# Linear attention and two expert layers on one core: zero products ahead of the first pair, its k in two transfers, and the negative sign first

## The chip, the cores and the metric

One core of one Trainium2 chip runs the whole program. The metric is device time in microseconds (us) of one execution. The engines are TensorE (PE, with PEld its weight loads), VectorE (DVE), ScalarE (ACT), GpSimd (POOL) and SyncE (SP), whose queue issues nearly all transfers.

## The reference

q, k and v have 4 batches of 8 heads, 576 tokens and 64 columns; w_phi has 64 rows and 128 columns.

```python
def phi(x):
    proj = np.einsum('bhsd,df->bhsf', x, w_phi)
    proj = proj - np.max(np.abs(proj), axis=-1, keepdims=True)
    return np.concatenate([np.exp(proj), np.exp(-proj)], axis=-1)
q_p, k_p = (phi(q), phi(k))
kv = np.einsum('bhsf,bhsd->bhfd', k_p, v)
z = np.sum(k_p, axis=2)
num = np.einsum('bhsf,bhfd->bhsd', q_p, kv)
den = np.einsum('bhsf,bhf->bhs', q_p, z)[..., None] + 1e-06
attn = num / den
...
h = x @ w_in                       # first layer, 2304 x 512 by 512 x 2048
x = np.maximum(0.01 * h, h) @ w_out
h = x @ w_in                       # second layer
out = (h * (1.0 / (1.0 + np.exp(-h)))) @ w_out
```

## The kernel before

The 32 heads are worked as 16 pairs, two heads beside each other on the 128 partitions. The first 8 pairs are "full": their products are in full float32. The later 8 are split into a high and a low part and made beside the first layer. The first layer goes over five tiles of 460 or 462 tokens (t) and over 16 blocks of hidden columns (c); each h is made of high and low parts by three products (emit_h, line 533) and goes into four output banks (emit_y, line 553). The second layer is made of seven products for each two-by-two block (lines 613 and 689).

A full pair goes through these steps. load_qk (line 110) and load_v issue on SP the transfers of kr (512 tokens of k), kt (its last 64 tokens), qr (q) and va (v). s_pk makes k's features with w_phi, two banks of two products each (line 180), and s_pkt those of the tail (line 195); each product leaves two records in the trace. k_features takes the largest absolute value (DVE, line 156) and subtracts it (line 157); then ACT makes exp(-x) into sign slot 1 (line 166) and exp(x) in place into sign slot 0 (line 167), for four token groups at once and, with the tail, for five. s_pq makes q's features (line 217), copies them to p (ACT, lines 223 and 225) and lets POOL find the largest value m over the partitions (line 227); s_eq subtracts it (DVE, line 239) and makes both exponentials of q (ACT, lines 243 and 244). These come in two parts of the tokens, 0 and 1. s_kv makes the key-value products of both signs, one of line 262 and eight of line 268 for each, and ACT copies the bank to KV (line 273). num_full makes the numerators and the denominator (line 302, in part 1 also line 305); DVE adds 1e-6 (line 311), takes the reciprocal (312) and makes x (313); PE transposes x (lines 316 and 320), and ACT and DVE split it into the first layer's high and low input (lines 287 and 126).

In between, the weights of the first layer are prepared: raw is a block of w_in or w_out as 64-bit words (line 411), narrowed by ACT (lines 420 and 421) and DVE (lines 422 to 425) and split into wih and wil, or wo (lines 429 and 126). Three buffers hold raw; two hold kr, three kt, qr and va. Four PSUM banks are called ps_a and four ps_y.

What sets the order: the program calls the steps by a table of due times, OFF0 for the full pairs, five units a pair, with prep_wi put in at four places (PRE). The framework that records the kernel then schedules all instructions and gives each engine a fixed order of its own. So a few instructions more can give every engine another order. A transfer has one of eight semaphores, DMAHW0 to DMAHW7, in turn; the one that takes a semaphore again waits until the transfer that had it has landed.

Of the kernel before, what the change touches and what calls it, by code (L numbers as in the profile page):

```python
# [8 lines left out]
F32 = mybir.dt.float32  # L9
# [10 lines left out]
def tile_linear_attention_ffn_ffn(ctx: ExitStack, tc: tile.TileContext, q, k, v, w_phi, w_in1, w_out1, w_in2, w_out2, out):  # L20


    nc = tc.nc
# [7 lines left out]
    S0 = 512  # L31
# [12 lines left out]
    gp = ctx.enter_context(tc.tile_pool(name="gp", bufs=2))  # L44
# [7 lines left out]
    def at(shape, dt, tag):  # L52
        return att_pool[0].tile(shape, dt, tag=tag, bufs=AB[0].get(tag, 1), name=tag)

    def ps(tag):

        return psp.tile([128, 512], F32, tag=tag, name=f"ps_{tag}")
# [3 lines left out]
    def aps(step):  # L61

        return ps("y" if PRO[0] and step in ("pq", "kv", "nt") else "a")
# [9 lines left out]
    def make_consts():  # L73
        for c in (slice(0, 2 * F), slice(2 * F, 3 * F + 128)):
            nc.scalar.dma_start(wc[:, c], w_phi[:, c])
        first = [const.tile([128, 2], F32, name=f"first{i}") for i in range(2)]
        nc.gpsimd.memset(first[0], 0.0)
        nc.gpsimd.partition_all_reduce(first[1], first[0], 128, bass_isa.ReduceOp.absmax)
# [30 lines left out]
    def load_qk(i):  # L109

        st = P[i]
        st["kr"] = at([128, S0], F32, "kr")
        st["kt"] = at([128, 128], F32, "kt")
        st["qr"] = at([128, S], F32, "qr")
        nc.sync.dma_start(st["kr"], k[i, :, 0:S0])
        nc.sync.dma_start(st["kt"], k[i, :, S0:])
        nc.sync.dma_start(st["qr"], q[i])

# [6 lines left out]
    def sub(out_, x, h):  # L125
        nc.vector.tensor_tensor(out_, x, h.bitcast(F32), op=ALU.subtract)  # L126

    def full(i):
        return i < NFULL
# [126 lines left out]
    def s_kv(i):  # L256
        st = P[i]
        ke, va = st["ke"], st["va"]
        pv = aps("kv")[:, 0 : 4 * NKV].rearrange("p (s j d) -> p s j d", s=2, j=2)
        vf = va.rearrange("p c d -> p (c d)")  # L260
        for s in range(2):
            nc.tensor.matmul(
                pv[:, s, :, 0 : D + 1], ke[:, 8, s, :], va[:, 8:10], start=True, stop=False, skip_group_check=True
            )
            for j in range(2):
                for c in range(4):
                    w = (4 * j + c) * (D + 1)
                    nc.tensor.matmul(  # L268
                        pv[:, s, j], ke[:, 2 * c + j, s, :], vf[:, w : w + NKV], start=False, stop=(j == 1 and c == 3), skip_group_check=True
                    )  # L270
        if full(i):
            st["KV"] = at([128, 2, 2, NNUM], F32, "KV")
            nc.scalar.activation(st["KV"], pv[:, :, :, 0 : NNUM], AF.Copy)
            return
        h, l = st["KVH"], st["KVL"] = at([128, 2, 2, 2, D], F32R, "KVH"), at([128, 2, 2, 2, D], F32R, "KVL")
        for j in range(2):
            kv_, z_ = pv[:, :, j, 0:D], pv[:, :, j, D : D + 1].to_broadcast([128, 2, D])
            for slot, sr in ((j, kv_), (1 - j, z_)):
                nc.scalar.activation(h[:, j, :, slot, :], sr, AF.Copy)
                sub(l[:, j, :, slot, :], sr, h[:, j, :, slot, :])  # L280
# [80 lines left out]
    def s_num(a):  # L361
        return lambda i: (num_full if full(i) else num_split)(i, a)

    W, WP = 8.0, 5.0
    fns = dict(
        lq=load_qk, lv=load_v, sp=s_split, pq0=s_pq(0), pq1=s_pq(1),
        pk0=s_pk(0), pk1=s_pk(1), pkt=s_pkt, eq0=s_eq(0), eq1=s_eq(1), kv=s_kv, num0=s_num(0), num1=s_num(1), fin0=s_fin(0), fin1=s_fin(1),
    )
    FIN = 16
# [19 lines left out]
    def run_att(until, tile_=None):  # L389
        while seq and (seq[-1][0] < until or (tile_ is not None and missing(tile_))):  # L390
            if seq[-1][1] == NFULL and AB[0] is ABUFS0:
                att0_ctx.close()
                att_pool[0] = att_ctx.enter_context(tc.tile_pool(name="att1", bufs=1))
                AB[0] = ABUFS1
            _, i, n_ = seq.pop()
            f = fns[n_]
            f(i)
# [76 lines left out]
    def prep_wi(layer, c):  # L474
        raw = load_wi(layer, c)
        h = wp.tile([128, KD, 128], F32R, tag="wih", bufs=NC, name="wih")
        l = wp.tile([128, KD, 128], F32R, tag="wil", bufs=NC, name="wil")
        split64(raw, h.rearrange("p k f -> p (k f)"), l.rearrange("p k f -> p (k f)"))
        wi[layer, c] = (h, l)
# [235 lines left out]
    def pace(s):  # L715

        return SLOW * min(s, NC) + FAST * max(0, s - NC)

    make_consts()
    for c in range(PRE):  # L720
        run_att(13.52 + 11.07 * c)
        prep_wi(0, c)
# [52 lines left out]
    for u, gs in GROUPS.items():  # L775
        for i, ps_ in enumerate(gs):
# [7 lines left out]
            if last:  # L784
                y = y3_ops(u, list(ps_))
# [87 lines left out]
```

## Time and profile before

| | us |
|---|---|
| median of 3 runs | 964.19 |
| lowest, highest | 962.32, 964.91 |
| the profiled execution | 963.19 |
| its span, first to last instruction | 961.4 |

The profile is of one execution. A row of the timeline gives start and length in us, the engine, the line, the tiles written and read, the number of merged records and, in brackets, how long the engine had stood idle and what ended that. The windows give, for a stretch, its length and the busy time of each engine with the number of instructions, then the clock that TensorE was granted (1.00 is 2.4 GHz), the mean busy share of the sixteen DMA engines and what they moved.

### The profile page before, as it was taken

The page shows a single profiled execution, that of the slowest core. Times are in us where ns is not written, and L with a number is a line of the kernel's source. Part 1 is how long each engine was busy: PE and PEld are TensorE (multiplying, and loading weights), DVE is VectorE, ACT ScalarE, POOL GpSimd, SP SyncE. Part 2 cuts the span into 40 slices and gives each one's busy share as a digit, 9 for nine tenths or more (in the row PEclk, how much of TensorE's full clock was granted, in tenths as well). Part 3 has the DMA queues.
Part 4 walks back from the last instruction along what each step waited for, and adds up shares of the span by engine and source line. Part 5 has one row for each costly group of instructions (what it writes and reads, how often), then busy time and mean ns, then how long its engine had stood idle before and what let it go on. Part 6 is the DMA issues. An engine that isn't in the chain of part 4 may idle for free.

```text
span 961.4 us, 15778 instructions
## 1 busy us (share of the span) xinstructions
PE 943.6 (98%) x5376; PEld 883.6 (92%) x5376; DVE 649.1 (68%) x1279; ACT 597.2 (62%) x1224; POOL 78.4 (8%) x56
## 2 busy tenths in 40 slices
PE   7999999999999999999999999999999999999998
PEld 6878888889999998888888999999999999999998
DVE  6677799986666655278777767778762595624853
ACT  6568687877777776466655556566554565544553
POOL 3434200201111111000000000000000000000000
PEclk9999999999999999999999999999999999999999
DMA  6333477874334232299999999896988778987784
GB/s 223 99 105 102 154 243 256 284 267 129 116 112 116 78 128 79 86 355 384 356 337 334 368 356 346 299 349 239 319 287 294 243 234 264 300 281 222 251 278 138
DMA packets 102384, 226.13 MB, mean 235 GB/s; under 512 B 15008, under 2 KB 24992, under 8 KB 102304
## 3 DMA queue, kind: packets, MB, share of 16 engines
q1 hardware_dynamic: 102016, 224.86, 69.9%
q8 instruction: 43, 0.70, 0.3%
q14 instruction: 37, 0.30, 0.1%
q10 hardware_dynamic: 288, 0.26, 0.1%
HBM read 177.82 MB, written 47.22 MB: 234 GB/s over the span
## 4 chain that ended last, share of the span: by engine, by line
PE 79%; DMA 8%; DVE 6%; ACT 4%; issue 1%; SPq 1%; DVEq 0%; ACTq 0%
PE ps_y L689 18%; PE ps_y L553 16%; PE ps_a L533 16%; PE ps_a L613 10%; PE ps_y L613 8%; DMA d<-rec 2%; PE ps_a L268 2%; PE ps_a L302 2%; DMA rec<-e 2%; PE ps_a L334 1%; PE ps_y L268 1%; DMA raw<-in_moe_w_in_dram 1%; DMA e<-d 1%; PE ps_a L180 1%; DMA w7s<-wst 1%
## 5 line engine op out<-in xcount | busy, mean ns | idle before, releaser
L689 PE MATMUL ps_y<-gt,ws 128*128 128x384 f32 x1008 | 177.2, 337 | 0.0
L689 PEld LDWEIGHTS ps_y<-gt,ws 128*128 128x128 f32 x1008 | 176.4, 188 | 0.1
L553 PE MATMUL ps_y<-gh,wo 128*128 128x460 f32 (+1 forms) x640 | 149.5, 372 | 2.2 <-DVE wo L126 1.3
L553 PEld LDWEIGHTS ps_y<-gh,wo 128*128 128x128 f32 x640 | 119.0, 188 | 16.6 <-ACT gh L429 1.9
L533 PE MATMUL ps_a<-xh,wih 128*128 128x460 f32 (+1 forms) x320 | 119.4, 373 | 0.8 <-ACT p L223 0.8
L533 PE MATMUL ps_a<-xl,wih 128*128 128x460 f32 (+1 forms) x320 | 118.9, 372 | 0.0
L533 PE MATMUL ps_a<-xh,wil 128*128 128x460 f32 (+1 forms) x320 | 118.7, 371 | 0.0
L613 PE MATMUL ps_a<-xs,ws 128*128 128x384 f32 x546 | 104.7, 338 | 0.1
L613 PEld LDWEIGHTS ps_a<-xs,ws 128*128 128x128 f32 x546 | 96.7, 188 | 0.8 <-issue 0.4
L227 POOL PARTITION_ALL_REDUCE m<-p x32 | 72.9, 2280 | 293.7 <-ACT p L223 212.4
L429 ACT ACTIVATE gt<-g 128x384 fp32r<-128x384 f32 x120 | 62.8, 524 | 51.3 <-PE ps_y L689 49.3
L126 DVE TENSOR_TENSOR gt<-g,gt 128x384 fp32r<-128x384 f32 x120 | 66.5, 555 | 34.4 <-ACT gt L429 33.5
L613 PE MATMUL ps_y<-xs,ws 128*128 128x384 f32 x462 | 88.5, 338 | 0.1
L613 PEld LDWEIGHTS ps_y<-xs,ws 128*128 128x128 f32 x462 | 81.7, 188 | 0.6 <-DVE g L589 0.5
L553 PE MATMUL ps_y<-gl,wo 128*128 128x460 f32 (+1 forms) x320 | 81.6, 372 | 0.0
L126 DVE TENSOR_TENSOR gl<-g,gh 128x460 fp32r<-128x460 f32 (+1 forms) x80 | 51.6, 646 | 30.6 <-ACT gh L429 26.1
L533 PEld LDWEIGHTS ps_a<-xh,wih 128*128 128x128 f32 x320 | 60.2, 188 | 7.4 <-ACT p L223 1.0
L553 PEld LDWEIGHTS ps_y<-gl,wo 128*128 128x128 f32 x320 | 60.2, 188 | 7.0
L536 ACT ACTIVATE g<-ps_a 128x460 f32<-128x460 f32 (+1 forms) x80 | 44.1, 552 | 35.9 <-PE ps_a L533 35.1
L533 PEld LDWEIGHTS ps_a<-xh,wil 128*128 128x128 f32 x320 | 60.1, 188 | 6.8
L533 PEld LDWEIGHTS ps_a<-xl,wih 128*128 128x128 f32 x320 | 60.2, 188 | 6.0
L429 ACT ACTIVATE gh<-g 128x460 fp32r<-128x460 f32 (+1 forms) x80 | 46.6, 584 | 8.1 <-PE ps_y L553 7.1
(142 smaller groups left out, 1552.3 us busy)
## 6 DMA issues: line engine op xcount, KB each, us to landing
ws<-w7s SPq DMA_DIRECT2D x336, 256.0 KB, 3.7
wo<-wos SPq DMA_DIRECT2D x64, 512.0 KB, 5.2
w7s<-wst SPq DMA_DIRECT2D x48, 512.0 KB, 6.0
raw<-in_moe_w_in_dram SPq DMA_DIRECT2D x32, 512.0 KB, 5.3
raw<-in_moe_w_out_dram SPq DMA_DIRECT2D x32, 512.0 KB, 5.8
wos<-wo SPq DMA_DIRECT2D x16, 512.0 KB, 4.3
va<-in_v_dram SPq DMA_DIRECT2D x16, 325.0 KB, 4.1
qr<-in_q_dram SPq DMA_DIRECT2D x16, 288.0 KB, 3.9
```

Of the source, the lines that this page charges most:

```text
L126: nc.vector.tensor_tensor(out_, x, h.bitcast(F32), op=ALU.subtract)
L180: nc.tensor.matmul(o, st["kr"][:, cs], BDF.rearrange("p j f -> p (j f)"), start=True, stop=True)
L227: nc.gpsimd.partition_all_reduce(m, p, 128, bass_isa.ReduceOp.absmax)
L268: nc.tensor.matmul(pv[:, s, j], ke[:, 2 * c + j, s, :], vf[:, w : w + NKV], start=False, stop=(j == 1 and c == 3), skip_group_check=True)
L302: nc.tensor.matmul(pb[:, w : w + NNUM], e[:, s, cs], KV[:, s, j], start=(s == 0), stop=(s == 1))
L334: nc.tensor.matmul(o, lhs, st[m, a][:, s, j * w : (j + 1) * w], start=(n == 0), stop=(n == 5))
L429: nc.scalar.activation(h, f, AF.Copy)
L533: nc.tensor.matmul(ph, a[:, kk, :], b_[:, kk, :], start=(m == 0), stop=(m == 3 * KD - 1))
L536: nc.scalar.activation(g, ph, AF.Prelu, alpha=0.01)
L553: nc.tensor.matmul(Y[t][d][:, 0:n], a[:, ds_], b_, start=(c == 0 and m == 0), stop=(c == NC - 1 and m == 1), skip_group_check=True)
L613: nc.tensor.matmul(bank[b_], w[:, a, kk], x[:, c, kk], start=(first and m == 0), stop=(m == 5), skip_group_check=True)
L689: nc.tensor.matmul(bank[b_][db], w[:, a, db], t[:, c], start=(first and p == 0 and m == 0), stop=(p == NP - 1 and m == 2), skip_group_chec ...
```

## The change

Three edits. The first pair's kr comes in two transfers of 256 tokens each. s_kv makes sign slot 1, exp(-x), first. And a new function, called behind the constants and ahead of everything else, lets DVE set a tile z to zero and PE multiply z by itself three times into a bank of ps_y that nothing reads.

```diff
-        nc.sync.dma_start(st["kr"], k[i, :, 0:S0])
+        for c in (slice(0, 256), slice(256, S0)) if i == 0 else (slice(0, S0),):
+            nc.sync.dma_start(st["kr"][:, c], k[i, :, c])
         nc.sync.dma_start(st["kt"], k[i, :, S0:])
         nc.sync.dma_start(st["qr"], q[i])
...
-        for s in range(2):
+        for s in (1, 0):
             nc.tensor.matmul(
                 pv[:, s, :, 0 : D + 1], ke[:, 8, s, :], va[:, 8:10], start=True, stop=False, skip_group_check=True
             )
...
+    def wake():
+
+        z, bank = gp.tile([128, 256], F32, tag="g", name="z", bufs=2), ps("y")
+        nc.vector.memset(z, 0.0)
+        for _ in range(3):
+            nc.tensor.matmul(bank[:, 0:256], z[:, 0:128], z, start=True, stop=True)
+
     make_consts()
+    wake()
```

The schedule comes out new on every engine up to the end of the first tile of the first layer and in places behind it; from the second layer on it is the same. Lines of the new kernel stand one higher than those named above, so that 181 is line 180 of before. Three places follow.

SP's queue from its first row, before; DMAHW names the semaphore waited for, PE a buffer that PE must free:

```order
L115 DMA kr<-in_k_dram 128x512
L116 DMA kt<-in_k_dram 128x128
L117 DMA qr<-in_q_dram 128x576
L123 DMA va<-in_v_dram 128x650
L115 DMA kr<-in_k_dram 128x512
L116 DMA kt<-in_k_dram 128x128
L117 DMA qr<-in_q_dram 128x576 [waits DMAHW0_49]
L123 DMA va<-in_v_dram 128x650 [waits DMAHW1_49]
L116 DMA kt<-in_k_dram 128x128 [waits DMAHW2_49]
L117 DMA qr<-in_q_dram 128x576 [waits DMAHW3_49]
L123 DMA va<-in_v_dram 128x650 [waits DMAHW4_49]
L115 DMA kr<-in_k_dram 128x512 [waits DMAHW5_49,PE_49]
L411 DMA raw<-in_moe_w_in_dram 128x1024 [waits DMAHW6_49]
```

The same place now, from the first v on:

```order
L124 DMA va<-in_v_dram 128x650
L116 DMA kr<-in_k_dram 128x512
L117 DMA kt<-in_k_dram 128x128 [waits DMAHW0_49]
L118 DMA qr<-in_q_dram 128x576 [waits DMAHW1_49]
L124 DMA va<-in_v_dram 128x650 [waits DMAHW2_49]
L117 DMA kt<-in_k_dram 128x128 [waits DMAHW3_49]
L116 DMA kr<-in_k_dram 128x512 [waits DMAHW4_49,PE_49]
L118 DMA qr<-in_q_dram 128x576 [waits DMAHW5_49]
L124 DMA va<-in_v_dram 128x650 [waits DMAHW6_49]
L412 DMA raw<-in_moe_w_in_dram 128x1024 [waits DMAHW7_49]
```

The waits begin one transfer earlier, pair 2's kr has moved ahead of its qr and va, and raw has the same transfers ahead of it as before.

ACT from an exponential of pair 1's first k groups to the copy of pair 0's KV, before (t_247 and r_248 belong to the first block of weights, t_552 and r_553 to the second):

```order
L166 ACTIVATE ke<-ke 128x4x128
L420 ACTIVATE t_247<-raw 128x512
L421 ACTIVATE r_248<-raw 128x512
L167 ACTIVATE ke<-ke 128x4x128
L243 ACTIVATE qh<-m 128x512
L244 ACTIVATE qh<-m 128x512
L420 ACTIVATE t_552<-raw 128x512
L421 ACTIVATE r_553<-raw 128x512
L273 ACTIVATE KV<-ps_y 128x384
```

The same place now (t_254 and r_255 the first block, t_559 and r_560 the second):

```order
L168 ACTIVATE ke<-ke 128x4x128
L421 ACTIVATE t_254<-raw 128x512
L244 ACTIVATE qh<-m 128x512
L245 ACTIVATE qh<-m 128x512
L224 ACTIVATE p<-ps_y 128x256 x2
L422 ACTIVATE r_255<-raw 128x512
L274 ACTIVATE KV<-ps_y 128x384
L421 ACTIVATE t_559<-raw 128x512
L422 ACTIVATE r_560<-raw 128x512
```

Pair 1's exponential moved ahead of the weights, the second block behind KV, and two copies of pair 1's p ahead of it.

DVE and PE up to the transposes of pair 0's first part. DVE before, from the second block's conversion to x:

```order
L422 TENSOR_SCALAR t_552<-t_552 128x512
L423 TENSOR_SCALAR t_552<-t_552 128x512
L424 SCALAR_TENSOR_TENSOR t_552<-raw,t_552 128x512
L239 TENSOR_TENSOR m<-p,m 128x640
L126 TENSOR_TENSOR wil<-r_248,wih 128x512
L425 ISA r_553<-t_552,r_553 128x1024
L311 TENSOR_SCALAR d<-ps_a 128x4
L156 TENSOR_REDUCE km<-ps_a 128x1
L312 RECIPROCAL d<-d 128x4
L157 TENSOR_TENSOR ke<-ps_a,km 128x128
L313 TENSOR_TENSOR x<-ps_a,d 128x256
```

DVE now, from the split of the first block:

```order
L127 TENSOR_TENSOR wil<-r_255,wih 128x512
L312 TENSOR_SCALAR d<-ps_a 128x4
L157 TENSOR_REDUCE km<-ps_a 128x1
L426 ISA r_560<-t_559,r_560 128x1024
L313 RECIPROCAL d<-d 128x4
L158 TENSOR_TENSOR ke<-ps_a,km 128x128
L240 TENSOR_TENSOR m<-p,m 128x512
L240 TENSOR_TENSOR m<-p,m 128x640
L314 TENSOR_TENSOR x<-ps_a,d 128x256
```

PE before, from pair 0's second half of the key-value products:

```order
L262 MATMUL ps_y<-va,ke 128x2x65
L268 MATMUL ps_y<-va,ke 128x112 x8
L217 MATMUL ps_y<-qr,wc 128x256 x2
L302 MATMUL ps_a<-KV,qh 128x96 x8
L195 MATMUL ps_a<-wc,kt 128x128
L180 MATMUL ps_a<-wc,kr 128x256 x4
L302 MATMUL ps_a<-KV,qh 128x96 x8
L305 MATMUL ps_a<-KV,qh 128x130 x2
L316 MATMUL ps_y<-wc,x 128x128 x2
```

PE now, from pair 1's first query products:

```order
L218 MATMUL ps_y<-qr,wc 128x256 x2
L263 MATMUL ps_y<-va,ke 128x2x65
L269 MATMUL ps_y<-va,ke 128x112 x8
L303 MATMUL ps_a<-KV,qh 128x96 x8
L196 MATMUL ps_a<-wc,kt 128x128
L181 MATMUL ps_a<-wc,kr 128x256 x4
L317 MATMUL ps_y<-wc,x 128x128 x2
```

Pair 0's second numerator (lines 302 and 305) no longer stands ahead of the transposes but behind pair 1's key-value products, and on DVE pair 1's subtraction (128x512) has moved ahead of x.

## Rows read from the trace of the kernel before

**Rows 1.** The page's first part: busy us, share of span, instructions.

```profile
PE 943.6 (98%) x5376; PEld 883.6 (92%) x5376; DVE 649.1 (68%) x1279; ACT 597.2 (62%) x1224; POOL 78.4 (8%) x56
```

**Rows 2.** Windows by stage: length, busy PE, PEld, DVE, ACT, POOL, clock, DMA, GB/s.

```profile
4.30:112.00 107.70, 102.37 (x757) 87.87 (x758) 83.68 (x178) 76.35 (x173) 42.19 (x34) 1.00 0.40 130
112.00:215.00 103.00, 100.30 (x526) 89.98 (x526) 93.90 (x180) 78.99 (x148) 7.73 (x3) 1.00 0.78 259
215.00:480.00 265.00, 263.20 (x1491) 241.68 (x1490) 165.43 (x328) 180.10 (x378) 27.83 (x13) 1.00 0.53 175
480.00:961.40 481.40, 477.71 (x2607) 464.07 (x2605) 306.09 (x594) 260.42 (x526) 0.00 (x0) 1.00 0.85 287
```

**Rows 3.** Line 180 up to 40 us: duration in ns, minimum, median, maximum.

```profile
L180 PE MATMUL ps_a<-wc,kr x32: 379/379/796, 4.3 to 34.9; 128*128 128x256 f32 x32
```

**Rows 4.** Timeline of PE in the opening.

```profile
4.30 3.78 PE L180 MATMUL ps_a<-wc,kr 128*128 128x256 f32 x8 [4.30 <-DMA wc<-in_w_phi_dram]
...
12.10 0.49 PE L262 MATMUL ps_y<-va,ke 128*128 128x130 f32 x2 [0.43 <-ACT ke L167]
...
14.19 0.40 PE L262 MATMUL ps_y<-va,ke 128*128 128x130 f32 x2
...
16.30 0.70 PE L217 MATMUL ps_y<-qr,wc 64*128 64x256 f32 x4
18.17 2.02 PE L302 MATMUL ps_a<-KV,qh 128*128 128x96 f32 x16 [1.17 <-ACT KV L273]
...
20.29 1.89 PE L180 MATMUL ps_a<-wc,kr 128*128 128x256 f32 x8
22.48 2.00 PE L302 MATMUL ps_a<-KV,qh 128*128 128x96 f32 x16 [0.31 <-ACT wih L429]
...
24.79 0.38 PE L316 MATMUL ps_y<-wc,x 128*128 128x128 f32 x2
```

**Rows 5.** Timeline of SP's queue: start, length of the issue.

```profile
3.05 0.43 SPq L116 DMA_DIRECT2D kt<-in_k_dram  x1
4.28 0.33 SPq L117 DMA_DIRECT2D qr<-in_q_dram  x1
...
8.12 0.33 SPq L115 DMA_DIRECT2D kr<-in_k_dram  x1
8.49 0.43 SPq L411 DMA_DIRECT2D raw<-in_moe_w_in_dram  x1
```

**Rows 6.** Chain that ended last, up to 60 us: start, length, what.

```profile
0.72 3.54 DMA wc<-in_w_phi_dram
...
8.49 5.30 DMA raw<-in_moe_w_in_dram
```

**Rows 7.** A window of the opening, columns as in rows 2.

```profile
3.00:13.80 10.80, 9.06 (x41) 7.08 (x42) 6.60 (x12) 5.41 (x13) 3.82 (x2) 1.00 1.02 358
```

**Rows 8.** Timeline of ACT and DVE in the opening, in order of time.

```profile
13.81 0.68 ACT L420 ACTIVATE t<-raw 128x512 f32<-128x512 f32 x1 [0.89 <-DMA raw<-in_moe_w_in_dram]
...
17.22 0.43 DVE L422 TENSOR_SCALAR t<-t 128x512 f32<-128x512 f32 x1 [0.25 <-ACT t L420]
17.63 0.49 ACT L273 ACTIVATE KV<-ps_y 128x384 f32<-128x384 f32 x1
...
18.00 0.66 ACT L223 ACTIVATE p<-ps_y 128x256 f32<-128x256 f32 x2
...
19.48 1.66 DVE L126 TENSOR_TENSOR wil<-r,wih 128x512 fp32r<-128x512 f32 x1
...
22.25 0.41 DVE L313 TENSOR_TENSOR x<-ps_a,d 128x256 f32<-128x256 f32 x1
...
23.18 0.68 DVE L126 TENSOR_TENSOR wil<-r,wih 128x512 fp32r<-128x512 f32 x1
...
23.78 0.68 DVE L239 TENSOR_TENSOR m<-p,m 128x512 f32<-128x512 f32 x1
```

**Rows 9.** Waits of PE, 112 to 240 us: total, times, longest, in us.

```profile
PE ps_y L553 <- DVE wo L126: 1.3, 1, 1.3
```

## The prediction

> **What bounds the kernel now.** I read the page's busy times first, then busy time by stage, then TensorE's waits, then the opening instruction by instruction. TensorE (PE) is busy for 98% of the span [rows 1], so nothing but PE's own unfilled time and slow time can be won. By stage [rows 2] PE is unfilled for 5.33 us of the opening (107.70 less 102.37, from the first product to the end of the eight full pairs), 2.70 us from 112 to 215, 1.80 us from 215 to 480 and 3.69 us after it. All that the change can move lies in the first two stages, where the other engines are close behind: VectorE (DVE) works 93.90 of the 103 us from 112 to 215.
>
> In the opening the same product on line 180 takes 379 ns at the median and 796 ns at the most [rows 3]. The slow ones are the first: the eight records of pair 0 take 3.78 us, those of pair 2 take 1.89 us [rows 4]. So pair 0's k features cost 1.89 us more than later ones, at half the rate.
>
> Whether these 1.89 us are on the path is the question, and the chain of waits answers it. It goes from w_phi's transfer into these first products, but after 8.10 us it leaves PE: raw, the first expert weight, is issued at 8.49 us and takes 5.30 us [rows 6]; ScalarE (ACT) starts on it at 13.81 us, the copy KV of pair 0 stands seven instructions behind that in ACT's queue, at 17.63 us, and PE's first numerator waits 1.17 us for KV, at 18.17 us [rows 4, 8]. So from 8.5 to 22.5 us the opening is paced by a transfer and by the queues of ACT and DVE, not by PE.
>
> **The change, part by part.** *Three products of zeros.* Four products of this shape took 3.78 us at the slow rate, so three take 2.84 us. They need only the memset; DVE has nothing else to do before w_phi lands and the queues open at 0.72 us, so the products end near 4 us, before w_phi lands at 4.26 us [rows 6]. Cover: the wait for w_phi. If they ran past it, PE would be late by the excess. They could give back anything from 0 to 1.89 us of PE's time on pair 0; I take 1.89 us, since later products of the shape hold at 379 ns.
> The granted-clock column reads 1.00, the 2.4 GHz level, over the whole opening [rows 2], though the first products took twice the time of later ones; so here the durations tell the level: 796 ns beside 379 ns is about what 1.2 against 2.4 GHz would make. The Trainium skill (TensorE: Matmul & The Clock Gate, Part 1, "What's actually happening") says that the slow clock is the default and that activity of TensorE releases it; by that the zeros give the whole 1.89 us to pair 0, and its caveat under "Seeing it yourself", that recorded clock events cannot be relied on, agrees with the column here.
>
> *k in two halves.* PE's first wait is ended by w_phi [rows 4], and k is there by then, so an earlier half of k gains nothing. It adds one issue, about 0.4 us (8.12 to 8.49 us is one), to everything behind it on SP. More important: eight transfers can be open at once. Before, pair 1's kt is issued at 3.05 us and qr waits until 4.28 us, w_phi's landing [rows 5]; now kt waits too. On SP, pair 2's kr waited for PE until 8.12 us, with raw 0.37 us behind it [rows 5]. PE will free that buffer 1.89 us sooner, but raw now waits for the landing of pair 1's kr (DMAHW7 in the order above), which before was DMAHW6 of the same transfer. And from 3 to 13.8 us all sixteen DMA engines are full, share 1.02 at 358 GB/s [rows 7], with the same bytes ahead of raw. So raw lands at 13.8 us as before; I allow 0.5 us either way.
>
> *Negative sign first.* Pair 0's key-value products waited 0.43 us for the positive exponential [rows 4]; the negative one is made first, so this goes. The scheduler puts pair 1's query products between the halves (0.70 us by the row at 16.30). PE then ends pair 0's key-value products no earlier than 16.30 - 1.89 - 0.43 + 0.70 = 14.7 us. That is early enough in any case, since what follows waits for ACT.
>
> *The moved instructions on ACT.* Before, seven instructions lie between 13.81 and 17.63 us, 0.55 us each. Now, six: the first conversion of raw, two exponentials of q, two copies of p, the second conversion. Four at 0.55 us and 0.66 us for the two copies [rows 8] make 2.84 us: KV starts at 16.65 us, and by the old distance of 0.54 us PE's numerator at 17.2 us. Gain so far 18.17 - 17.2 = 1.0 us, out of 2.3 us that PE had gained.
>
> *The moved instructions on DVE and PE.* The second conversion of the weights now starts behind KV: KV's 0.5 us and 0.55 us for its first step on ACT put DVE's work on it at 17.7 us instead of 17.22 us. From there to x of pair 0 it was 22.25 - 17.22 = 5.03 us [rows 8]; one subtraction for pair 1 (0.68 us long, 0.6 us apart) is now ahead of x. That gives 17.7 + 5.03 + 0.6 = 23.3 us, if the split of the weights again takes 1.66 us, and 22.3 us if it takes 0.68 us as the next one of its kind does [rows 8]. I take 22.3 us, the more usual duration. x takes 0.41 us, so PE's transposes start at 22.7 us (at the most 23.75 us).
> PE is there earlier: the numerator at 17.2 us and 4.00 us to the end of pair 2's k features (18.17 to 22.48 us before, less the 0.31 us of wait in it) give 21.2 us. It waits 1.5 us for x. Before, x was 2 us old when PE came to it, because pair 0's second numerator, 22.48 to 24.79 us, stood between [rows 4]. This numerator, 2.31 us, now comes after pair 1's key-value products, so it is still owed. Done work compared at the transposes: 22.7 + 2.31 = 25.0 us against 24.79 us. PE is 0.2 us late; with the other bound 1.3 us late. A new wait has eaten the 1.89 us, the 0.43 us and what the earlier KV brought.
>
> *Behind that.* Up to 112 us the eight pairs repeat with the same products; their waits are short and in other places in the new order, and I count them at nothing, with 1 us either way. In the stage from 112 us PE waits once for 1.3 us on DVE's split of a weight [rows 9]. In the new order of ACT two more weights are begun before the first tile's gh, and DVE has about one narrowing more behind it there; that fills time in which DVE waits now, and I give the change these 1.3 us, between 0 and the stage's whole 2.70 us.
>
> **The sum.** The profiled execution took 963.19 us, of which the span is 961.4 us. It lies 1.0 us under the median of 964.19 us, which I start from. +0.2 - 1.3 = -1.1 us: 963.1 us.
>
> **The rivals.** *A, the gain goes through: faster.* If raw lands earlier by what PE frees the k buffer earlier, 1.89 us, then KV, the weights and x all move with it and nothing eats the gain: 964.19 + 0.2 - 1.89 - 1.3 = 961.2 us, and with all 2.70 us of the second stage 959.8 us. For it: SP did wait for PE at 8.12 us, right ahead of raw [rows 5]. Against it: the DMA engines are full until raw has landed [rows 7], and raw still waits for another landing.
> *B, the clock falls in the new waits: slower.* PE now stands still for up to 2.5 us ahead of 17.2 us and for 1.5 us from 21.2 us. The longest wait after the start that the trace shows is 1.17 us, and products behind it are at full rate [rows 4]. If a longer one lets the clock fall, it costs what the first products cost, 1.89 us. Once, without the gain at 112 us: 964.19 + 0.2 + 1.89 = 966.3 us; twice 968.2 us. It decides from a wait beyond 1.17 us on; for it speaks that the engine began slow after standing still, against it that both waits are far shorter than the 4.30 us of the start.
> *C, the zeros don't raise the clock.* Then pair 0 stays at 3.78 us, but the chain through raw is the same: 964.2 us, with the 1.3 us or without.
>
> **How the numbers follow.** Forecast 0.47, C 0.08: both within 0.3% (2.9 us, about what a measurement of this kernel can tell from no change). A 0.33, since its mechanism begins in a wait that is there, and the order of every engine is new up to the first tiles. B 0.12. So faster 0.33, same 0.55, slower 0.12. The predicted time is the forecast's, 963.1 us; its own bounds are 963.1 - 1.4 (the rest of the 2.70 us) - 1.0 = 960.7 us and 963.1 + 1.1 (the later x) + 1.3 (nothing at 112 us) + 1.0 = 966.5 us. The range 959.6 to 967.2 us takes in nearly all of A and the milder half of B.
>
> **What would show it.** Right: pair 0's eight records at about 1.9 us; raw landing near 13.8 us; PE idle before the first numerator on KV and, newly, before the first transposes on x at about 22.7 us; PE's transposes of pair 0 done near 23 us with the second numerator behind pair 1's key-value products. Wrong: records of 796 ns in pair 0 (C); raw landed before 13 us and x before 21.5 us (A); records at twice their time behind 17 or 22 us (B); or a difference that arises only after 112 us, which I priced from one wait alone.

## The result, and the profile after

The changed kernel takes 975.04 us (median of four runs, 974.73 to 976.9) where the kernel before takes 964.25 us on the same chip: 1.0119 times as long, 95% interval 1.010 to 1.0138. It is slower by 10.8 us; the prediction was 963.1 us, between 959.6 and 967.2 us. The profiled execution took 974.73 us, its span 973.0 us. (Of the changed kernel every line from 116 up to the new function has a number one higher than before: L303 is the numerator's line 302, L274 KV's 273, L181 the k features' 180.)

Where the 11.6 us of the two spans lie is read from windows that end at the same piece of work: the first product of the first expert layer, the first product of the second, the end. First the kernel before, then after (columns as in [rows 2]).

```profile
0.00:111.75 111.75, 102.12 (x757) 87.62 (x757) 83.68 (x178) 77.40 (x173) 42.85 (x40) 1.00 0.40 131
111.75:568.00 456.25, 451.75 (x2438) 411.00 (x2438) 325.02 (x635) 308.07 (x618) 35.56 (x16) 1.00 0.68 229
568.00:961.40 393.40, 389.71 (x2185) 384.98 (x2184) 240.40 (x466) 211.69 (x434) 0.00 (x0) 1.00 0.82 272
```

```profile
0.00:120.35 120.35, 108.29 (x757) 92.40 (x757) 85.09 (x174) 75.07 (x169) 40.86 (x40) 0.96 0.39 125
120.35:578.40 458.05, 453.55 (x2445) 411.97 (x2445) 326.98 (x641) 309.53 (x621) 36.34 (x16) 1.00 0.67 227
578.40:973.00 394.60, 389.64 (x2185) 385.00 (x2183) 240.41 (x466) 211.57 (x434) 0.00 (x0) 1.00 0.82 272
```

The opening, up to the first expert product, is 8.60 us longer. The middle is 1.80 us longer, all of it work: TensorE (PE) is idle for 4.50 us in both, and has seven more products to do there, which the opening still owed. The second layer is 1.20 us longer, a wait for a transfer. So the loss is made in the first 120 us. There PE is idle for 12.06 us in place of 9.63, although it now starts on w_phi's products earlier and fills 2.93 us of the start with zeros; and its granted clock, 1.00 before, is 0.96.

The opening can be cut once more, at pair 6's first key-value product. Up to there the work done is the same in both, but for the zeros and four records of line 306, some 0.6 us, that the changed kernel still owes. First the kernel before, then after:

```profile
0.00:93.64 93.64, 84.66 (x608) 71.88 (x609) 67.18 (x142) 63.42 (x143) 34.15 (x32) 1.00 0.43 136
93.64:111.75 18.11, 17.46 (x151) 15.74 (x149) 16.50 (x38) 13.98 (x31) 8.71 (x9) 1.00 0.28 105
```

```profile
0.00:94.44 94.44, 87.53 (x611) 74.10 (x611) 67.26 (x139) 59.82 (x135) 32.02 (x31) 0.98 0.43 135
94.44:120.35 25.91, 20.75 (x149) 18.30 (x147) 17.83 (x36) 15.24 (x36) 8.84 (x9) 0.87 0.27 90
```

Of the 8.60 us only 0.80 arise up to there. The last stretch of the opening, pairs 6 and 7, makes 7.80, with 149 records in place of 151: PE is idle for 5.16 us in place of 0.65, and the clock is 0.87.

PE's waits over the whole run (total, times, longest); the first line is the kernel before, the others the changed one:

```profile
PE ps_a L302 <- ACT KV L273: 2.7, 5, 1.2
PE ps_a L303 <- ACT KV L274: 8.4, 8, 4.0
PE ps_y L554 <- DVE gl L127: 1.8, 1, 1.8
```

The opening of PE's timeline, which answers to [rows 4], up to pair 0's transposes; then the one long wait, at pair 6 (start, length, engine, line, tile, shape, records, idle before and what ended it):

```profile
1.17 2.93 PE L725 MATMUL ps_y<-z 128*128 128x256 f32 x6 [1.17 <-DVE z L723]
3.89 2.36 PE L181 MATMUL ps_a<-wc,kr 128*128 128x256 f32 x8
...
17.26 2.63 PE L303 MATMUL ps_a<-KV,qh 128*128 128x96 f32 x16 [1.54 <-ACT KV L274]
...
23.29 0.44 PE L317 MATMUL ps_y<-wc,x 128*128 128x128 f32 x2 [0.37 <-DVE x L314]
...
103.90 3.73 PE L303 MATMUL ps_a<-KV,qh 128*128 128x96 f32 x16 [3.99 <-ACT KV L274]
```

The numerator's 16 records take 2.02 us at full rate [rows 4]; here they take 2.63 and 3.73 us. The granted clock, the number before the last two of each window, says why:

```profile
18.00:20.00 2.00, 2.00 (x14) 2.00 (x14) 1.93 (x5) 0.86 (x2) 0.62 (x2) 0.62 0.06 13
20.00:22.00 2.00, 2.00 (x7) 1.64 (x7) 2.00 (x7) 0.61 (x2) 0.00 (x0) 0.52 0.11 33
22.00:23.00 1.00, 0.92 (x5) 0.47 (x3) 1.00 (x3) 0.97 (x3) 0.00 (x0) 1.00 0.00 0
...
104.00:110.00 6.00, 6.00 (x28) 5.22 (x30) 2.18 (x8) 1.01 (x4) 0.00 (x0) 0.50 0.75 258
110.00:111.00 1.00, 0.85 (x4) 0.00 (x0) 1.00 (x3) 0.50 (x3) 0.00 (x0) 0.67 0.07 29
111.00:112.00 1.00, 0.56 (x5) 0.56 (x6) 0.49 (x2) 1.00 (x4) 0.00 (x0) 1.00 0.03 12
```

Behind each of the two longest waits the clock falls to 0.50, the lower level (1.2 GHz): some 1.2 us into the work at the first place, at once at the second. It comes back after some 3.5 and 6.8 us of work. At half rate for a time, half of that time is lost: 2.00 x 0.38 + 2.00 x 0.48 = 1.7 us at the first place, 6.00 x 0.50 + 1.00 x 0.33 = 3.3 us at the second.

What makes the wait of 3.99 us stands on ScalarE (ACT) and VectorE (DVE), in order of time, with GpSimd's (POOL) reductions beside them:

```profile
96.97 2.66 POOL L228 PARTITION_ALL_REDUCE m<-p  x1 [6.46 <-ACT p L226]
97.49 1.32 DVE L423 TENSOR_SCALAR t<-t 128x512 f32<-128x512 f32 x1 [0.24 <-ACT t L421]
98.84 1.06 DVE L424 TENSOR_SCALAR t<-t 128x512 uint32<-128x512 uint32 x1
100.20 2.23 POOL L228 PARTITION_ALL_REDUCE m<-p  x1 [0.57 <-ACT p L224]
100.55 1.66 DVE L127 TENSOR_TENSOR wil<-r,wih 128x512 fp32r<-128x512 f32 x1
102.12 0.68 DVE L426 CUSTOM_DVE_ANT_0 r<-t,r 128x1024 uint16<-128x1024 uint16 x1
102.84 0.63 ACT L430 ACTIVATE wo<-r 128x512 fp32r<-128x512 f32 x1 [2.73 <-DVE r L426]
103.37 0.47 ACT L274 ACTIVATE KV<-ps_y 128x384 f32<-128x384 f32 x1
```

ACT's order has the copy wo<-r ahead of KV. That copy waits 2.73 us for DVE's last step on a weight, and KV, whose products PE had finished by 98.6 us, waits behind it; PE's numerator waits for KV. In the kernel before KV stands behind the same copy, but DVE was done with the weight at 97.35 us, a little ahead of pair 6's products (97.81 us):

```profile
97.38 0.63 ACT L429 ACTIVATE wo<-r 128x512 fp32r<-128x512 f32 x1 [1.47 <-DVE r L425]
```

### The profile page after: what moved, and what is told of

The parts are those of the page before. It is cut to its first block, busy times and chain, and to the rows that moved or that the text cites. A ratio compares the mean times of both kernels' runs of the same rounds, so it can differ in the third digit from the quotient of the medians.

```text
span 973.0 us, 15795 instructions
## 1 busy us (share of the span) xinstructions
PE 951.5 (98%) x5382; PEld 889.4 (91%) x5382; DVE 652.5 (67%) x1280; ACT 596.2 (61%) x1224; POOL 77.2 (8%) x56
## 4 chain that ended last, share of the span: by engine, by line
PE 79%; DMA 8%; ACT 6%; DVE 5%; issue 1%; SPq 1%; DVEq 0%; ACTq 0%
PE ps_y L690 18%; PE ps_y L554 16%; PE ps_a L534 16%; PE ps_a L614 10%; PE ps_y L614 8%; PE ps_a L303 3%; PE ps_a L269 2%; DMA d<-rec 2%; PE ps_y L269 1%; DMA rec<-e 1%; DMA raw<-in_moe_w_in_dram 1%; DMA kr<-in_k_dram 1%; PE ps_a L335 1%; DMA e<-d 1%; DMA w7s<-wst 1%
```

## The experiments

Each run computes the whole of the reference. Ratios are against the kernel before on the same chip, with 95% intervals. e1 to e4 make one or two of the three edits and leave the order of the instructions to the scheduler, which makes a new one for each. From e5 on the order is held: a table of the order that one kernel got is written into another, and each instruction of an engine is tied to the one ahead of it in that table, by edges that set the order alone and wait for nothing.

```
+for a, b in zip(seq, seq[1:]):
+    tc.add_manual_dep(by[e][b], by[e][a].name, NoSync edge)
```

**e1, the zeros alone.**

```
+z, bank = gp.tile([128, 256], F32, tag="g", name="z", bufs=2), ps("y")
+nc.vector.memset(z, 0.0)
+for _ in range(3):
+    nc.tensor.matmul(bank[:, 0:256], z[:, 0:128], z, start=True, stop=True)
```

> The kernel before with the three zero products alone. TensorE's order is that of before, three products apart, so theory O (the sign edit brings a new order on ScalarE and TensorE, in which pair 6 waits 4.0 us for KV, and the clock falls in two of the waits) expects 964 us within 2: pair 0's first products shorter by some 1.4 us, the later chain through raw unchanged, and perhaps one fall of the clock near 17 us, since the wait for KV grows from 1.17 to some 2.6 us (+1.6 us). Rival Z (the zero products are to blame: early work followed by standing still makes the clock fall and costs what the change cost) expects 970 to 976 us and a granted clock of 0.995 as in the changed kernel.

962.24 us, ratio 0.999 (0.9979 to 1.0001). PE's timeline:

```profile
4.23 3.54 PE L180 MATMUL ps_a<-wc,kr 128*128 128x256 f32 x8
...
12.57 0.49 PE L262 MATMUL ps_y<-va,ke 128*128 128x130 f32 x2 [1.48 <-ACT ke L167]
```

The zeros end at 4.10 us, and yet pair 0's first products take 3.54 us, hardly less than the 3.78 us without them [rows 4]; with all three edits they took 2.36 us, in e4 2.70 us. What the zeros give here is between 0.24 and 1.42 us. PE's order is that of the kernel before, and the gain ends in a wait of 1.48 us.

**e2, the halves alone.**

```
-nc.sync.dma_start(st["kr"], k[i, :, 0:S0])
+for c in (slice(0, 256), slice(256, S0)) if i == 0 else (slice(0, S0),):
+    nc.sync.dma_start(st["kr"][:, c], k[i, :, c])
```

> The kernel before with pair 0's k in two transfers and nothing else. TensorE's order is that of before. Theory O expects 964 us within 1.5: w_phi ends the first wait in any case. Rival H (the split shifts the eight open transfers and delays raw, and with it the opening) expects raw to land later than 13.8 us by 1 us or more and 966 us or more.

963.83 us, ratio 1.0001 (0.9989 to 1.0013): nothing, as the prediction had it.

**e3, the negative sign first alone.**

```
-for s in range(2):
+for s in (1, 0):
```

> The kernel before with the negative sign first and nothing else. The order of ScalarE and TensorE is new from pair 0 on. Theory O expects most of the loss, 970 to 976 us, with a long wait for KV at a late pair. Rivals Z and H expect 963 to 965 us here, since neither zeros nor a split are in it.

966.47 us, ratio 1.0031 (1.0021 to 1.0042). A loss, but a quarter of the whole, and outside both expected ranges. There is no wait of 4 us; the waits for KV are 3.4 us in five times, and behind the longest the clock falls (PE's timeline, then a window):

```profile
18.48 3.49 PE L302 MATMUL ps_a<-KV,qh 128*128 128x96 f32 x16 [1.48 <-ACT KV L273]
```

```profile
19.00:22.00 3.00, 3.00 (x15) 3.00 (x15) 3.00 (x4) 1.34 (x3) 1.93 (x1) 0.50 0.00 0
```

**e4, zeros and halves.** The two edits above together.

> Zeros and halves without the sign edit: TensorE's order is nearly that of before (two places differ). Theory O expects 964 us within 2, the whole loss gone; Z and H expect the loss to stay, 970 us or more. If the zeros alone let the clock fall once near 17 us, this run shows the same.

960.32 us, ratio 0.997 (0.9958 to 0.9983): faster by 0.3%, with the clock at 1.00, and below both expected ranges. So the loss of the three edits, +1.19%, is not the sum of their own (-0.1%, 0.0% and +0.31%). Either the sign costs much more beside the others, or the order does that the scheduler makes of all three.

**e5 and e6 part the sign from the order.** e5 has all three edits in the order that e4 got; e6 has e4's two edits in the order that the changed kernel got. In both only the two signs of a pair's key-value products change places against the kernel whose order it is.

> All three edits, but every engine's instructions are held in the order in which zeros and halves alone (960.3 us) put them; only the two signs change places inside a pair's key-value products. Theory O (the edits are harmless, the loss of 10.8 us is in the order that the scheduler made of all three): 958.3 to 961.3 us, granted clock 1.00, no wait of L303 for KV above 1.6 us. Rival S (negative first costs time by itself, by later copies of KV or a wait of the products): 963 us or more.

> Zeros and halves, positive sign first as before the change, but every engine's instructions held in the order of the changed kernel. Theory O: 974 to 977 us, the wait of about 4 us for KV at 100 to 104 us still there, the clock falling behind it. Rival S (the sign itself costs): 966 us or less, and no long wait.

e5: 960.98 us, ratio 0.9945 (0.9929 to 0.9962). e6: 978.07 us, a little above the expected 974 to 977, ratio 1.0127 (1.0098 to 1.0156). With e4 and the changed kernel this is a table of two by two: in e4's order 0.997 with the positive sign first and 0.9945 with the negative, in the changed kernel's order 1.0127 and 1.0119. The sign moves the time by less than the intervals can tell; the order moves it by 1.6 to 1.7%. Rival S falls. e5 does all that the change does and is faster than the kernel before and than the changed kernel.

e6's long wait and what is behind it are like those of the changed kernel:

```profile
104.18 3.31 PE L303 MATMUL ps_a<-KV,qh 128*128 128x96 f32 x16 [3.24 <-ACT KV L274]
```

**e7 and e8 take the long wait apart**, both in the changed kernel's order. e7 exchanges two instructions of ACT:

```
 L224 p<-ps_y
+L274 KV<-ps_y
 L430 wo<-r
-L274 KV<-ps_y
```

e8 leaves the waits and gives PE something to do in them (of the three kernels with this edit, e8, e12 and e14, the lines behind it are two higher):

```
+for _ in range({0: 5, 6: 13}.get(i, 0) if a == 0 else 0):
+    nc.tensor.matmul(pb[:, 390:512], ident, ident[:, 0:122], start=True, stop=True)
```

> The changed kernel with its own order held, and one exchange on ACT: the copy of pair 6's KV (L274) stands ahead of wo's copy (L430), which waits 2.73 us for DVE. Theory Q (the copy only stood behind a copy that waited for DVE): KV is copied at about 100.1 instead of 103.4, the numerator starts at about 100.6 instead of 103.9, no clock fall behind it; transposes of pair 6's first half then wait for x, since DVE's order is as it was, so that 2.9 to 6.5 of the 7.1 us (3.99 wait and 3.15 slow products) come back: 968.5 to 972.2 us. Rival R (the wait only moves, to x behind wo on DVE): 973.5 to 975.5 us.

> The changed kernel with its own order held, and products of the identity into unused columns of the numerator's bank just ahead of the first numerator of pair 0 (5 of 122 columns) and of pair 6 (13 of 122): TensorE works through the two waits of 1.54 and 3.99 us. Theory C (of the loss, the fallen clock is a share of its own): the granted clock stays 1.00 at 18 to 22 us and at 104 to 111 us, the numerator of pair 6 takes 1.9 instead of 3.5 us, the waits stay as long, and 2.5 to 4.8 us come back: 970 to 972.8 us. Rival D (the slow products were no loss, what follows waits as long anyway): 974 us or more, with the clock at 1.00.

e7: 972.09 us, ratio 1.0066 (1.0043 to 1.0088). PE at pair 6:

```profile
100.63 2.02 PE L303 MATMUL ps_a<-KV,qh 128*128 128x96 f32 x16 [0.58 <-ACT KV L274]
...
103.72 0.41 PE L317 MATMUL ps_y<-wc,x 128*128 128x128 f32 x2 [0.82 <-DVE x L314]
...
105.02 0.44 PE L317 MATMUL ps_y<-wc,x 128*128 128x128 f32 x2 [0.63 <-DVE x L314]
```

The numerator starts 3.27 us earlier and runs at full rate; 1.45 us of that comes back as waits for x, since DVE's order is unchanged. By ratio 0.53%, 5.1 us, of the loss goes. In the traces the stretch from pair 6's first key-value product to the first expert product shrinks by 4.67 us, from 25.91 to 21.24. Theory Q holds: the long wait was KV standing behind a copy that waited for DVE. Why DVE was late is another question, for the last section.

e8: 971.45 us, ratio 1.0057 (1.0035 to 1.008), granted clock 1.00.

```profile
101.03 3.06 PE L299 MATMUL ps_a<-wc 128*128 128x122 f32 x26
105.06 2.02 PE L305 MATMUL ps_a<-KV,qh 128*128 128x96 f32 x16 [0.97 <-ACT KV L274]
```

The wait is as long as before (from 101.0 to 105.06 us, now filled but for its last 0.97 us), and what follows runs at full rate: 0.62%, 6.0 us with some 3 us of uncertainty, of the loss goes. The traces say it more closely: the stretch from pair 6's first key-value product to the first expert product takes 23.13 us in place of 25.91, 2.78 us less, within the 2.5 to 4.8 us expected. So the fallen clock was a share of its own, as theory C says: some 2.8 of the 4.7 us that e7 brings in the same stretch. The two gains are not to be added: without the wait there is no fall behind it.

**e11 tries a tempting reason**, that PE lacks a piece of work to put into the wait: in the kernel before and in e4, the second numerator of the pair before stands nearer to it. In the changed kernel's order:

```
-L303 (second half of pair 5) x8
 L263, L269 (pair 6) x18
 L218 x2
+L303 (second half of pair 5) x8
 L306 x2
 L303 (pair 6) x8
```

> The changed kernel with its own order held, and one exchange on TensorE: the eight products (L303) of pair 5's second half stand behind pair 6's key-value products and not ahead of them, so that they lie between those products and the numerator that waits for KV. Theory Q (KV is late because ACT's copy ahead of it waits for DVE; TensorE has no work of its own to put there): the numerator of pair 6 starts at 103.4 to 104.2 us as before, TensorE idles as long in all, 973.5 to 976.5 us. Rival P (the missing cover on TensorE was the cause): 1.9 us less of waiting and no clock fall, 969.5 to 972.5 us.

974.5 us, ratio 1.0116 (1.0086 to 1.0145).

```profile
104.09 3.73 PE L303 MATMUL ps_a<-KV,qh 128*128 128x96 f32 x16 [3.45 <-ACT KV L274]
```

No change in the trace: the same work ahead of KV or behind its products leaves the start of the numerator at 104 us, since ACT and DVE set it. Theory Q again. The times alone would not have told: the trace is of the longest of four executions (977.06 us, mean granted clock 0.991), and two others took 972.64 and 972.12 us at 0.998, beside rival P's range.

**e9 and e10 cut the order in two** at pair 6's key-value products: e9 has e4's order ahead of the cut and the changed kernel's behind it, e10 the reverse.

> All three edits; what the changed kernel does ahead of pair 6's key-value products (316 matrix products, 136 ACT and 137 DVE instructions) stands in the order that e4 and e5 had, everything from there on in the order of the changed kernel. Theory L (most of the loss stands at and behind pair 6): the wait of 3.5 to 4.5 us for KV stays, only the first clock fall and some of the 0.58 us waits go: 970 to 974.5 us. Rival F (the loss is spread over the pairs ahead of it): 962 to 968 us.

> The mirror of e9: the changed kernel's own order up to pair 6's key-value products, the order of e4 and e5 from there on. Theory L: the long wait and its clock fall go, the fall at 18 to 22 us and six waits of 0.2 to 0.6 us for KV stay: 962 to 967.5 us. Rival F: 969 to 974 us.

e9: 964.94 us, ratio 1.0024 (1.0008 to 1.004). e10: 968.09 us, ratio 1.0048 (1.0032 to 1.0064). From the changed kernel's 1.0119 to e5's 0.9945 it is 1.74%; the first part alone gives back 0.95%, the second alone 0.71%. e9 lies in rival F's range, e10 between the two. But these shares are of the way to e5, which is faster than the kernel before. From e5's trace to the changed kernel's, 5.24 us lie ahead of pair 6's first key-value product (89.20 against 94.44 us) and 7.34 behind it; against the kernel before it was 0.80 and 7.80. So what has to be explained does stand at and behind pair 6, as theory L has it, and what e5 gains ahead of it is a better order there than the kernel before had. The two parts do not simply add up either. The stretch behind pair 6's first key-value product is in the same order in e9 and in the changed kernel, and yet it takes 21.82 us in e9 in place of 25.91:

```profile
89.50:111.32 21.82, 19.18 (x149) 16.75 (x147) 15.64 (x34) 13.36 (x30) 7.91 (x9) 0.92 0.31 107
```

Each mixed order also makes a clock fall of its own. In e9 the wait at pair 6 is 1.47 us, and in e10 PE waits only 0.17 us for KV but 1.21 us for x, and the clock falls all the same. A window of e9, then PE's timeline and a window of e10:

```profile
98.00:101.00 3.00, 3.00 (x17) 2.21 (x17) 1.90 (x7) 1.01 (x4) 0.00 (x0) 0.53 0.98 320
```

```profile
102.97 0.44 PE L317 MATMUL ps_y<-wc,x 128*128 128x128 f32 x2 [1.21 <-DVE x L314]
...
105.45 3.57 PE L303 MATMUL ps_a<-KV,qh 128*128 128x96 f32 x16
```

```profile
104.00:110.00 6.00, 6.00 (x30) 5.96 (x29) 4.00 (x14) 4.28 (x9) 2.05 (x1) 0.50 0.40 158
```

**e12 asks what the first fall cost**: e7 with the five products of e8 ahead of pair 0's numerator.

> e7 (the changed kernel's own order, KV of pair 6 copied ahead of wo) with the five products of the identity ahead of pair 0's numerator from e8: both clock falls and the long wait are gone, what is left of the loss against e5 are the six or seven waits of 0.2 to 0.6 us for KV and the later order. In the time of the kernel before on the same chip (about 964): theory H (the fall at 18 to 22 us cost little, since the slow products stood where TensorE would have waited for x; the wait for x comes back at 1.3 to 2 us): within 1 us of e7, 969.5 to 971.5 us. Rival G (the slow products were a loss in full): 1.6 to 2 us below e7, 967.5 to 969.5 us.

971.23 us, ratio 1.0078 (1.0053 to 1.0103), not below e7. PE in the opening:

```profile
18.05 2.02 PE L305 MATMUL ps_a<-KV,qh 128*128 128x96 f32 x16 [0.81 <-ACT KV L274]
...
24.02 0.44 PE L319 MATMUL ps_y<-wc,x 128*128 128x128 f32 x2 [1.97 <-DVE x L316]
```

Theory H holds: the numerator is back at 2.02 us, and PE waits 1.97 us for x in place of 0.37. From the numerator's start to the transposes it is 6.03 us in the changed kernel, with the fall, and 5.97 us here, without it. The slow products of the opening had stood where PE would have waited anyway. That fall cost next to nothing, the one at pair 6 most of the 3.3 us worked out above. The traces of e7 and e12 have another fall, from some 204 to 207 us, which by the granted clock costs each some 1.7 us that the changed kernel does not lose there; the last section comes back to it.

**What the pairs ahead of pair 6 lose against e5.** ACT's copies of KV show a part of it, in the changed kernel and in e5:

```profile
58.42 0.49 ACT L274 ACTIVATE KV<-ps_y 128x384 f32<-128x384 f32 x1 [1.28 <-PE ps_a L306]
```

```profile
55.20 0.49 ACT L274 ACTIVATE KV<-ps_y 128x384 f32<-128x384 f32 x1 [2.20 <-PE ps_y L269]
```

In e5 the copy is released by its own pair's products (L269). In the changed kernel L306 releases it at pairs 1, 3, 4 and 7, the second numerator of the pair before: KV has one buffer, which that numerator reads, and in this order it stands behind the next pair's products. PE then waits 0.58 us for the copy. From the first copy of KV to pair 6's first key-value product it takes 77.72 us in the changed kernel (16.72 to 94.44) and 73.18 us in e5 (16.02 to 89.20). e13 gives KV a second buffer in the changed kernel's order, e14 does the same to e12:

```
-st["KV"] = at([128, 2, 2, NNUM], F32, "KV")
+st["KV"] = at([128, 2, 2, NNUM], F32, "KV") if i % 2 == 0 else gp.tile([128, 384], F32, tag="o", ...)
```

> The changed kernel with its own order held; KV of pairs 1, 3, 5 and 7 goes into a tile of its own, so that KV has two buffers. Theory K (in this order the copy KV stands behind the second numerator of the pair before, L306, which reads the only KV buffer; so TensorE waits 0.58 us for every such copy): the waits of 0.58 us at about 32, 59, 74 and 118.5 us go or fall under 0.2 us, KV's copies are no longer released by L306, 1.2 to 2.6 us come back: against the kernel before at about 964 us, 972 to 974 us. Rival A (the copies stand behind other work in ACT's queue, the buffer is free in time): the same waits, 974.5 to 976.5 us.

> e12 with two KV buffers: the long wait, both clock falls and, by theory K, the waits of 0.58 us are gone, all in the changed kernel's own order. Theory K: 1.2 to 3 us under e12 (971.2), 968 to 970 us where the kernel before takes about 964, the copies of KV 13.0 to 13.5 us apart from pair to pair in place of 13.8. Rival A: as e12, 970.5 to 972 us.

e13: 976.09 us, ratio 1.0117 (1.0087 to 1.0148). e14: 970.74 us, ratio 1.0053 (1.0036 to 1.007). In the trace theory K holds: in both, the waits of 0.58 us at pairs 1, 3, 4 and 7 are gone, and no copy of KV is released by L306. The same distance, 77.72 us, is 76.55 us in e13, and 75.94 us in e14 where e12 has 77.66: the second buffer is worth 1.2 and 1.7 us there, of the 4.5 us that this order loses to e5. In the time it is not shown: both runs lie in rival A's ranges and above K's, e13 is where the changed kernel is, and e14 lies 0.25% under e12, with intervals that overlap. e14's trace, of the longest of its five executions, shows where the gain went: behind pair 6's first key-value product e14 takes 23.44 us where e12 takes 21.19. PE comes earlier to pair 6, waits there four times for 0.54 to 0.89 us within 8 us, and the clock falls behind them (timeline, then a window):

```profile
104.95 0.80 PE L263 MATMUL ps_y<-va,ke 128*128 128x130 f32 x2 [0.70 <-ACT p L226]
105.55 3.60 PE L269 MATMUL ps_y<-va,ke 128*128 128x112 f32 x16
```

```profile
106.00:108.00 2.00, 2.00 (x11) 2.00 (x11) 0.00 (x0) 2.00 (x4) 0.75 (x1) 0.50 0.87 334
```

The 16 records of 3.60 us take 1.94 us at full rate. Of the 10 us between e14 and e5 (1.0053 and 0.9945) this fall takes some 3 us. The rest stays open as to single causes: e5 and e6 show that it is in the order, and no one wait in e14 is long enough to hold it.

## Why the prediction was wrong, point by point

**The opening was followed rightly, up to pair 0's transposes.** The zeros ended at 4.10 us (near 4 us), raw reached ACT at 14.03 us (13.8, with 0.5 us either way), KV was copied at 16.72 us (16.65), the numerator started at 17.26 us (17.2), the transposes at 23.29 us (22.7, at the most 23.75), behind x and without pair 0's second numerator. The halves brought nothing, as e2 shows. Three sizes were off. The zeros gave pair 0's products 1.42 us in the changed kernel and 0.24 us in e1 where 1.89 us were taken; that three products are enough for the whole was a step of the prediction's own. By the prediction's comparison of done work PE is 0.8 us late at the transposes (23.29 + 2.31 = 25.60 against 24.79 us) and not 0.2. And PE waited 0.37 us and not 1.5 us for x, because it came there late at the lower clock.

**Rival B came about, and its price was misjudged in both directions.** The clock did fall in a wait longer than 1.17 us, at 17.26 us, as that rival had it. The 1.89 us that it put on such a fall were about what the slow products took, but e12 shows that they cost next to nothing there: the wait for x took their place. The same hidden-or-not question that the prediction asked of every other term it did not ask of the clock.

**The step that failed is "Behind that. Up to 112 us [...] I count them at nothing, with 1 us either way".** The opening came out 8.6 us longer. Up to pair 6 the sentence held: the changed kernel is 0.80 us late at pair 6's first key-value product and owes some 0.6 us of work there, hardly more than the 0.8 us of pair 0's transposes. But pairs 6 and 7, which the sentence takes in as well, lost 7.80 us: PE was idle for 4.5 us more and lost 3.3 us to the lower clock. The sentence reasoned that the products are the same; but the order was new on every engine, and it was the order that had to be read. On ACT, pair 6's KV stands right behind a copy of wo, which in the trace of before already waited for DVE, 1.47 us at pair 6 and 1.60 us later, when PE had other work. With the clock behind it this wait is the largest piece: taking it away brought 4.67 of the 7.80 us (e7), keeping the clock up through it 2.78 (e8). What is left in e7 are five waits of 0.58 to 0.82 us in that stretch: 3.31 us of idle time against 0.65 in the kernel before. That the wait would grow to 4 us could not be read off the order alone: DVE came late with the weight as well. In PE's order the second numerator is behind the next pair's products in several pairs; the prediction saw this for pair 0 and booked it as work that is still owed, but not that the same numerator holds KV's only buffer. That cost 1.2 to 1.7 us in the trace (e13, e14), not against the kernel before, but against an order as good as e5's.

**The 1.3 us of gain from 112 us on did not come.** PE's idle time between the first product of each layer is 4.50 us before and 4.50 us after. The wait on DVE for wo went; one of 1.8 us on DVE for gl came.

**The chances.** Slower had 0.12, for rival B alone. Nothing was set aside for a new order that is worse as such, although the text said of rival A that the order of every engine is new. e4 and e5 show that the draw can also be a good one: the same edits in another order are 0.55% faster than before, so that the order decides the sign of this change.

## What to carry to other kernels

Where a scheduler reorders every engine after a small edit, the edit's own cost is the smaller part: compare the two orders over the whole stage, and look on each engine for an instruction that many wait for and that now stands behind one that itself waits, and for a single buffer whose last reader has moved behind its next writer. Part an edit from its order by running the edit in the old order and the old code in the new one; two runs settled here what three single edits had left confused. Price a clock fall like any other delay, by what would have been waited for in its place. And measure where a loss arises against the kernel before, between two ends of the same work: against the best order found, what that order gains looks like a part of the loss.

## What the runs showed of the hardware

**The same wait lets the clock fall in one run and not in another.** The plainest case is a wait for gl in the first layer, in e7 and then in the changed kernel:

```profile
202.43 1.11 PE L554 MATMUL ps_y<-gl,wo 128*128 128x462 f32 x4 [1.83 <-DVE gl L127]
```

```profile
207.33 1.11 PE L554 MATMUL ps_y<-gl,wo 128*128 128x462 f32 x4 [1.82 <-DVE gl L127]
```

Behind it the clock fell in e7 and e12 (1.83 us) and held in the changed kernel (1.82), e8 (1.83), e9 (1.80) and e13 (1.82). Elsewhere it fell behind waits of 1.47 us (e9, pair 6), 1.48 (e3), 1.54 (the changed kernel), 1.55 (e10, pair 0) and 1.97 us (e11, pair 0), behind 1.21 us in e10 and behind four waits under 0.9 us in e14. It held behind 1.46 (e4, for x), 1.48 (e1), 1.48 (e5, for x), 1.52 (e9, pair 0) and 1.97 us (e12, for x). The length of a single wait does not tell which. Executions of one kernel differ too: in e9's ten the mean granted clock goes from 0.994 (967.7 us) to 1.00 (962.34 us), so a trace shows the falls of one execution. The Trainium skill (TensorE: Matmul & The Clock Gate, Part 1, "What's actually happening") says that the clock follows how busy the engine has lately been, watched on a schedule that is not tied to the kernel; mixed outcomes for one length of wait would be expected from that, but no run here shows the schedule. After a fall the products ran at half rate for 3 to 7 us of unbroken work before the clock came back, and in e11 longer still.

**The granted-clock column does not show a slow start.** In e1 pair 0's records take up to 796 ns, about twice the 379 ns of later ones, from 4.23 us on, with the column at 1.00; later falls are in it.

**DVE slows down beside POOL's reductions.** At 97.49, 98.84 and 100.55 us, beside reductions over partitions from 96.97 to 99.63 and 100.20 to 102.43 us, three DVE instructions on 128x512 took 1.32, 1.06 and 1.66 us; the same lines a little earlier or later take 0.43, 0.42 and 0.68 us. That is 2.5 us more, about the 2.73 us that wo's copy waited for DVE. It is no single case. In the traces of the kernel before and of the changed one, up to 150 us, the conversions L423 and L424 of 128x512 (422 and 423 before) take 0.41 to 0.43 us wherever no such reduction runs beside them, and 0.42 to 1.32 us beside one; the subtraction L158 (157 before), which reads a PSUM bank, stays at 0.67 to 0.69 us beside one. The Trainium skill (SBUF — State Buffer, "Who interferes with whom") says that VectorE and GpSimd share one pair of ports, as a lock that blocks the other until the instruction ends. The rows agree that the two disturb each other, and differ in that the three DVE instructions end inside the reductions' recorded spans or 0.3 us behind one, slowed rather than blocked for its length. No run here took the reductions away, so this cause is argued, not shown.
